# A top-k attention with two expert layers: the mask moves from VectorE to ScalarE and GpSimd, ahead of the exponential

## The chip, the cores and the metric

The kernel runs on one core of a Trainium2 chip. The core has TensorE (matrix products), VectorE, ScalarE and GpSimd (elementwise work), and SyncE, which issues the DMA transfers. Every engine works through its own instructions in the order in which they were written down; semaphores make it wait for others. The metric is device time in microseconds, of which less is better.

## The reference

Attention over q, k and v of shape (4, 8, 576, 64), in which each query keeps its 32 largest scores, then two expert layers on the 2304 tokens of 512 numbers:

```python
scores = scale * np.matmul(q, k.transpose(0, 1, 3, 2))
kth = np.partition(scores, -top_k, axis=-1)[..., -top_k:-top_k + 1]
scores = np.where(scores >= kth, scores, -1000000000.0)
scores = scores - np.max(scores, axis=-1, keepdims=True)
attn = np.exp(scores)
attn = attn / (np.sum(attn, axis=-1, keepdims=True) + 1e-09)
x = np.matmul(attn, v)                        # -> (2304, 512)
h = np.maximum(x @ w_in1, 0.0);  y = h * h @ w_out1
h = y @ w_in2;  out = (h * np.clip(h + 3.0, 0.0, 6.0) / 6.0) @ w_out2
```

The four weight matrices have 512 x 2048 or 2048 x 512 numbers and arrive as 64-bit words.

## The kernel before

**Numbers.** Every operand of a product is split into two f16 parts, a high and a low one, after a scaling by a power of two; each product is done as three (high-high, high-low, low-high). The scale of a matrix needs its largest column norm first: products of the matrix with itself (line 428), a reduction on VectorE (line 448), a transpose and a spread on TensorE (lines 471, 478). Then each slab of 128x512 is scaled and split, for the first, second and most of the third matrix by products with a diagonal on TensorE (lines 536, 542) and copies on ScalarE, for the rest by ScalarE and GpSimd (lines 518 to 524). The first and third matrix have four reductions, the second and fourth one. Before that VectorE turns 64-bit words into f32 (lines 362 to 365), and GpSimd adds the low bits (line 412). Slabs are loaded into space that later holds other matrices, so a load waits until the slab before it in its place is converted.

**Attention.** There are 4 x 5 blocks of (batch, up to 128 tokens): four full ones and a half one of 64 a batch. A full block has 8 tiles, one for each head, a half one has 4 with two heads each: 144 tiles of 128x576 scores. `attend` writes down a tile's steps: score products (line 764), the copy S to SBUF on ScalarE (770), seven steps on VectorE that find the 32 largest (maximum of eight, line 778 and 786; replacement of these in W, line 783), a bias on GpSimd (790), the exponential on ScalarE (795), the mask on VectorE, which multiplies the exponential by S >= the 32nd value and sums the row (801), the high part wc on ScalarE (806), the low part on GpSimd (810, 811), a DMA transpose of both to wT (815) and the value products (829). `x_operand` divides by the sums and transposes a block into the buffer hl, with which the first layer starts. `q_prep` and `kv_prep` load and scale q, k and v; the scale comes from `norm_tasks`: squares summed on ScalarE (line 595), a sum over the partitions by a product with ones on TensorE (599), and a scale on VectorE (261 to 263).

**Layers.** The two half blocks of neighbouring batches are joined, so there are 18 units of 128 tokens. `group` writes down a quarter of a layer of a unit: products into hb (line 1075), Relu and square, or Relu and gate (1082 to 1090), the high part on ScalarE (1097), the low part on GpSimd (1100), second products (1110 in the first layer, 1118 in the second). `x2_operand` turns the first layer's result into the second's operand, in the same buffer hl, which is free only after the second layer.

**Order.** None of this order is written out by hand. `task` notes each step with its engine, an estimated cost, a key, what it waits for, and the buffers that it takes; `free` says whose end gives a buffer back. `Plan.run` plays the steps through with these estimates: an engine that is free takes the ready step with the smallest key for which all buffers are there, and that is the order in which instructions are written. `lat` is what the planner counts between a step's end and the start of those that wait for it (2.0 us after a step of SyncE). The keys come from constants at the end of the file: `AKEY` for the tile's steps on ScalarE and GpSimd, `GKEY` for the groups, `WKEY` for weight loads, `CKEY` for conversions, `SKEY` and `SPL` for splits, `QKV` for the loads of q, k and v.

Of the kernel before, what the change touches and what calls it, by code (L numbers as in the profile page):

```python
# [9 lines left out]
F32 = mybir.dt.float32  # L10
F16 = mybir.dt.float16
# [8 lines left out]
P = 128  # L20
# [12 lines left out]
class Plan:  # L33
# [29 lines left out]
    def free(self, name, owner, *users):  # L63
        e = [len(users), name, owner]
        for u in users:
            u.rel.append(e)
# [66 lines left out]
def tile_topk_attention_moe_moe2(  # L133
# [55 lines left out]
    def pool(name, n, shape, dtype, where=None):  # L189

        plan.pool(**{name: n})
        size[name] = (shape, dtype, where or sb)
# [20 lines left out]
    acc_t = ps.tile([P, 2, 512], F32, name="acc")  # L213
    plan.pool(acc0=1, acc1=1)
    pool("S", SBUFS, [P, S], F32)
    pool("W", 2, [P, S], F32)
    pool("E", 2, [P, S], F32)
    pool("wc", 2, [P, 2 * S], F16)
    pool("wT", 2, [P, 2 * S // P, P], F16)
    pool("kn", 1, [P, 4 * NCH * D], F16)  # L220
    pool("qT", 2, [P, 8, P], F16)
    pool("kT", 4, [P, 2 * NCH, P], F16)
# [2 lines left out]
    pool("qf", 1, [P, 4, D], F32)  # L225
    pool("x", XBUFS, [P, H, D], F32)
    pool("f", FBUFS, [P, 512], F32)
    pool("hl", 2, [P, 2, KD, 2 * P], F16)
    pool("ghl", GBUFS, [P, 2, 512], F16)
    pool("m", 3, [P, TOPK], F32, st)  # L230
    pool("sums", 2, [P, H], F32, st)
    pool("rv", 2, [P, H], F32, st)
    pool("scl", 3, [P, 2], F32, st)
    for name, n in (("nb", 2), ("ss", 6), ("sck", 1), ("scv", 1), ("scq", 2), ("qinv", 2), ("xy", 2), ("scx", 6),
                    ("px", 6), ("sc2", 4), ("p2", 2), ("r", 6), ("pm", 2), ("sm", 2), ("ca", 2), ("oc", 2)):
        scalar(name, n)
    scalar("wmx", 4)
# [19 lines left out]
    def scale_pair(y_ap, inv, add, sc):  # L257

        e = scalars[:, size["e"] + nexp[0] % 4:size["e"] + nexp[0] % 4 + 1].bitcast(I32)
        nexp[0] += 1  # L260
        nc.vector.tensor_scalar(e, y_ap.bitcast(I32), EXPMASK, 1, op0=ALU.bitwise_and, op1=ALU.logical_shift_right)
        nc.vector.tensor_scalar(sc.bitcast(I32), e, -1.0, EXP_S, op0=ALU.mult, op1=ALU.add)
        nc.vector.tensor_scalar(inv.bitcast(I32), e, 1.0, add, op0=ALU.mult, op1=ALU.add)
# [320 lines left out]
    def when(kkey):  # L584
        return first[kkey[1]] + 2.0 * kkey[2] if kkey[0] == "q" else first[first_of(order, kkey[1])] + kkey[2]

    def norm_tasks(tag, src, junk, n, cost, deps, alloc, inv, kkey, reads=(), writes=()):

        box = {}

        def square():
            for a_ in alloc:
                T[a_, kkey] = take(a_)
            box["ss"] = take("ss")
            nc.scalar.activation(junk(), src(), AF.Square, accum_out=box["ss"][0:n])

        def total():
            box["pn"] = take("misc", "pn" + tag)
            nc.tensor.matmul(box["pn"][:, 0:1], ones32[0:n, :], box["ss"][0:n], start=True, stop=True)

        def scale():
            box["sc"] = take("sc" + tag)
            scale_pair(box["pn"][:, 0:1], inv(), EXP_I, box["sc"])

        t1 = task("ACT", cost, (PREP, when(kkey)), square, deps=deps, alloc=["ss", *alloc], reads=reads, writes=writes)
        t2 = task("PE", 0.2, (0, when(kkey)), total, deps=[t1], alloc=["misc"])
        t3 = task("DVE", 0.34, (0, when(kkey)), scale, deps=[t2],
                  alloc=["sc" + tag] + (["qinv"] if tag == "q" else []))
        free("ss", t1, t2)
        free("misc", t2, t3)  # L610
        return box, t1, t3

    def kv_prep(which, b, hp, deps):
# [73 lines left out]
    def q_prep(i, half):  # L687

        b, j = order[i]
        n = nof[i]  # L690
        box = {}
        own = (i, half) == (0, 1)
        rd = []
        if own:
            box["f"], rd = region(32768 - 16 * D, 16 * D, F32)
        kkey = ("q", i, half)

        def load():
# [12 lines left out]

        bx, t1, t3 = norm_tasks("q", lambda: box["f"][0:n].rearrange("p h d -> p (h d)"),
                                lambda: T["kn", kkey][0:n].bitcast(BF16)[:, 0:4 * D], n, 0.4, [l], ["kn", "qT"],
                                lambda: T.setdefault(("qinv", kkey), None) or T.__setitem__(("qinv", kkey), take("qinv"))
                                or T["qinv", kkey], kkey, reads=rd)

        def scales():
            T["scl", kkey] = take("scl")
            for c in range(2):
                hp = 2 * half + c  # L720
                nc.gpsimd.tensor_scalar(T["scl", kkey][:, c:c + 1], kvinv[:, 0, b % 2, hp:hp + 1],
                                        T["qinv", kkey][:, 0:1], 0.125, op0=ALU.mult, op1=ALU.mult)

        def flip():
            nc.sync.dma_start_transpose(out=T["qT", kkey][:, :, 0:n],
                                        in_=T["kn", kkey][0:n, 0:16 * D])

        lows = split(4 * D, lambda: box["f"][0:n], [lambda a=a: qn()[0:n, :, 0, a, :] for a in range(2)],
                     [lambda a=a: qn()[0:n, :, 1, a, :] for a in range(2)], lambda: bx["sc"][0:n], SQ if b else SQ0,
                     ((PREP, when(kkey)), (1, when(kkey))), [t3], rd)  # L730
        t5 = task("POOL", 0.5, (0, when(kkey)), scales, deps=[t3] + [kT_task[b, 2 * half + c][1] for c in range(2)],
                  alloc=["scl"])
        t6 = task("SP", 1.0, (0, when(kkey)), flip, deps=lows)
        free("scq", t3, *lows)
        free("qinv", t3, t5)
        free("kn", t1, t6)
        if not own:
            free("qf", l, *lows)
        qT_task[i, half], qT_use[i, half] = (t1, t6), []
        scl_use[i, half] = (t5, [])  # L740
# [10 lines left out]
    def attend(s):  # L751
# [38 lines left out]
            nc.gpsimd.tensor_scalar(T["nb", s], T["m", s][:, 0:1], T["scl", ("q", i, half)][:, hp % 2:hp % 2 + 1],  # L790
                                    -1.0, op0=ALU.mult, op1=ALU.mult)

        def expo():
            T["E", s] = take("E")
            nc.scalar.activation(T["E", s], T["S", s], AF.Exp, bias=T["nb", s],  # L795
                                 scale=T["scl", ("q", i, half)][:, hp % 2:hp % 2 + 1])

        def mask():
            if t == 0:
                T["sums", i] = take("sums")  # L800
            nc.vector.scalar_tensor_tensor(T["E", s], T["S", s], T["m", s][:, TOPK - 1:TOPK], T["E", s],  # L801
                                           op0=ALU.is_ge, op1=ALU.mult, accum_out=T["sums", i][:, t:t + 1])

        def high():
            T["wc", s] = take("wc")
# [33 lines left out]
        for r in range(7):  # L839
# [2 lines left out]
            ops.append(prev)  # L842
        free("W", ops[1], ops[6])
        tn = task("POOL", 0.25, (0, s), bias, deps=[ops[0], scl_use[i, half][0]], alloc=["nb"])
        te = task("ACT", 0.76, (AKEY[1], s), expo, deps=[tn, before[1]], alloc=["E"])
        free("nb", tn, te)
        scl_use[i, half][1].append(te)
        tm = task("DVE", 0.815, (2, s + 0.7), mask, port=True, deps=[ops[6], te, mask_task.get((i, 0))],
                  alloc=["sums"] if t == 0 else [])
        mask_task[i, t] = tm  # L850
        free("S", tb, tm)
        free("m", ops[0], tm)
        th = task("ACT", 0.57, (AKEY[2], s), high, deps=[tm, before[2]], alloc=["wc"])
        tl = task("POOL", 1.38, (AKEY[3], s), low, deps=[th, before[3]])
        free("E", te, tl)
        tw = task("SP", 1.25, (0, s), flip, deps=[tl, before[4]], alloc=["wT"])
        free("wc", th, tw)
        tv = task("PE", 0.44 if len(hs) == 1 else 0.9, (2, s), av, deps=[tw, vv_task[b, hp][1], before[5]],
                  alloc=["av"] if t == 0 else [])
        av_tasks[i, t] = tv  # L860
        tile_tasks.append((ta, te, th, tl, tw, tv))
        free("wT", tw, tv)
        vv_use[b, hp].append(tv)

# [398 lines left out]
SBUFS = 3  # L1263
FBUFS = 2
XBUFS = 1
GBUFS = 3
PREFILL = 1
SKV = 'd'
SQ = 'a'
SKV0 = 'a'  # L1270
SQ0 = 'a'
GKEY = (4, 1.5)
AKEY = (0.5, 1, 3, 3.5)
SX = 'a'
SX0 = 'a'
XKEY = 1.5
NPOOL = (4, 4, 4, 4)
QKV = 0
WKEY = ((45.68, 1), (153.74, 0.1), (14.48, 0.1), (62.46, 0.1))
SPE = ('eeee', 'eeee', 'eeea', 'aaaa')  # L1280
SPL = (3.5, 1.5, 0.5)
ADD = (0.5, 1)
PREP = 1.5
VKEY = 3

CKEY = ((-3.61, 0.14), (-69.99, 3.36), (-31.64, 0.91), (-0.36, 1.29))
SKEY = (0, 100, 200, 300)

_INS = ["q", "k", "v", "moe_w_in", "moe_w_out", "moe2_w_in", "moe2_w_out"]
_OUTS = [((2304, 512), "float32")]  # L1290
# [24 lines left out]
```

## Time and profile before

| | |
|---|---|
| median of 3 runs | 1236.63 us (1236.08 to 1240.48) |
| the profiled execution's own time | 1238.58 us |
| its span, first to last instruction | 1236.8 us |
| TensorE products, busy | 1074.3 us, 87% |
| VectorE busy | 1058.9 us, 86% |
| ScalarE busy | 825.4 us, 67% |
| GpSimd busy | 663.8 us, 54% |
| mean granted TensorE clock | 0.947 |

The profile is of one execution. "PE" is TensorE's products and "PEld" its weight loads, "DVE" VectorE, "ACT" ScalarE, "POOL" GpSimd. Busy is the time in which at least one instruction of the engine ran. A line such as L801 is a line of the kernel. In a wait the engine, the instruction and the line that waited stand left of the arrow, and right of it what came last of that for which it waited.

### The profile page before, as it was taken

Reading aid. Unit: us, or ns where it says so; the run is one execution under the profiler, and the core shown is the slowest. Engines: PE = TensorE matmul, PEld = TensorE weight load, DVE = VectorE, ACT = ScalarE, POOL = GpSimd, SP = SyncE. Lnnn points to the kernel's source line nnn. Section 1 sums busy time; section 2 is a strip of 40 time slices with the busy share of each in tenths; the row PEclk is TensorE's granted clock in tenths of the full one; section 3 lists DMA queues with packets and bytes.
Section 4 is the critical chain, followed back from the end, with each engine's and each line's share of the span. In section 5 each row is a group of like instructions: output and inputs, shape, how many; then the busy total and the mean of one; then the engine's idle time right before and its main releaser. Section 6 shows DMA issues by size and latency. Waiting matters only on the chain.

```text
span 1236.8 us, 36708 instructions
## 1 busy us (share of the span) xinstructions
PE 1074.3 (87%) x14856; PEld 879.4 (71%) x14856; DVE 1058.9 (86%) x2463; ACT 825.4 (67%) x1580; POOL 663.8 (54%) x969
## 2 busy tenths in 40 slices
PE   2484389878989999999899999999998999999998
PEld 2332147577679769877887888788767868978885
DVE  5999999999978999999999999999868989999011
ACT  7677588769767668666766757576866666755422
POOL 5857846458654556554545555655544555545312
PEclk9676599998999999999899999999998999999999
DMA  9989744333454233344574323435433233433100
GB/s 209 268 247 265 228 101 115 71 55 55 96 113 93 53 63 70 66 71 82 89 109 72 68 56 71 55 64 98 97 59 73 54 66 73 65 49 58 22 2 18
DMA packets 276762, 112.47 MB, mean 91 GB/s; under 512 B 257521, under 2 KB 265713, under 8 KB 276593
## 3 DMA queue, kind: packets, MB, share of 16 engines
q1 hardware_dynamic: 276592, 110.14, 43.3%
q8 instruction: 116, 1.90, 0.6%
q14 instruction: 54, 0.43, 0.1%
HBM read 48.23 MB, written 4.72 MB: 43 GB/s over the span
## 4 chain that ended last, share of the span: by engine, by line
PE 42%; DVE 15%; ACT 10%; DMA 10%; issue 5%; POOL 5%; SPq 1%; POOLq 0%; DVEq 0%; ACTq 0%
PE hb L1075 16%; PE acc L1118 9%; PE acc L1110 8%; DMA wT<-wc 8%; DVE W L783 4%; DVE m L786 4%; PE av L829 3%; PE sp L764 3%; DVE E L801 2%; DVE m L778 2%; POOL wc L810 1%; ACT E L795 1%; POOL ghl L1100 1%; ACT x L896 1%; ACT S L770 1%
## 5 line engine op out<-in xcount | busy, mean ns | idle before, releaser
L1075 PE MATMUL hb<-hl,w 128*128 128x128 f16 x6912 | 455.8, 220 | 3.7 <-ACT r L1082 2.2
L1075 PEld LDWEIGHTS <-w 128*128 128x128 f16 x6912 | 415.7, 99 | 42.8 <-issue 6.2
L786 DVE MAX8 m<-W 128x8 f32<-128x576 f32 x432 | 314.8, 747 | 0.2
L1100 POOL TENSOR_TENSOR ghl<-r,ghl 128x512 f16<-128x512 f32 x144 | 172.7, 1201 | 193.3 <-ACT ghl L1097 141.9
L1110 PE MATMUL acc<-ghl,w 128*128 128x128 f16 x3456 | 242.0, 221 | 9.9 <-POOL ghl L1100 4.2
L810 POOL TENSOR_TENSOR wc<-E,wc 128x512 f16<-128x512 f32 x144 | 167.8, 1165 | 145.2 <-ACT wc L806 117.8
L1118 PE MATMUL acc<-w,ghl 128*128 128x512 f16 x864 | 234.3, 382 | 2.8 <-POOL ghl L1100 1.5
L1110 PEld LDWEIGHTS <-w 128*128 128x128 f16 x3456 | 212.8, 99 | 29.8 <-issue 14.0
L783 DVE MATCH_REPLACE8 W<-m,W 128x576 f32<-128x576 f32 x288 | 213.3, 742 | 0.0
L795 ACT ACTIVATE E<-S,scalars,scl 128x576 f32<-128x576 f32 x144 | 124.8, 867 | 85.9 <-POOL scalars L790 65.3
L801 DVE SCALAR_TENSOR_TENSOR E<-S,m,E 128x576 f32<-128x576 f32 x144 | 137.2, 952 | 0.1
L770 ACT ACTIVATE S<-sp 128x576 f32<-128x576 f32 x144 | 92.9, 645 | 53.8 <-DVE E L801 40.9
L764 PE MATMUL sp<-kT,qT 128*128 128x288 f16 (+1 forms) x640 | 102.4, 303 | 25.0 <-ACT S L770 21.0
L829 PE MATMUL av<-vv,wT 128*128 128x64 f16 (+1 forms) x2240 | 92.7, 197 | 33.7 <-DMA wT<-wc 32.8
L829 PEld LDWEIGHTS <-wT 128*128 128x128 f16 (+1 forms) x2240 | 81.2, 103 | 56.5 <-DMA wT<-wc 46.9
L1097 ACT ACTIVATE ghl<-r 128x512 f16<-128x512 f32 x144 | 89.8, 626 | 40.9 <-PE acc L1110 21.2
L778 DVE MAX8 m<-S 128x8 f32<-128x576 f32 x144 | 107.3, 746 | 4.9 <-ACT S L770 4.9
L783 DVE MATCH_REPLACE8 W<-m,S 128x576 f32<-128x576 f32 x144 | 106.8, 741 | 0.0
L1118 PEld LDWEIGHTS <-ghl 128*128 128x128 f16 x864 | 73.8, 99 | 45.2 <-issue 3.3
L806 ACT ACTIVATE wc<-E 128x576 f16<-128x576 f32 x144 | 97.7, 679 | 4.6 <-DVE E L801 4.5
L412 POOL TENSOR_TENSOR w<-w,stg 128x512 int32<-128x512 int32 x57 | 73.0, 1294 | 35.4 <-DVE w L365 23.6
L1090 DVE SCALAR_TENSOR_TENSOR r<-r,hb 128x512 f32<-128x512 f32 x72 | 48.9, 680 | 49.6 <-ACT r L1084 49.4
(128 smaller groups left out, 1343.2 us busy)
## 6 DMA issues: line engine op xcount, KB each, us to landing
w<-in_moe_w_in_dram SPq DMA_DIRECT2D x32, 512.0 KB, 4.8
w<-in_moe_w_out_dram SPq DMA_DIRECT2D x29, 512.0 KB, 4.8
out_dram<-o SPq DMA_DIRECT2D x16, 256.0 KB, 2.4
qf<-in_q_dram SPq DMA_DIRECT2D x31, 128.0 KB, 3.1
stg<-in_k_dram SPq DMA_DIRECT2D x12, 256.0 KB, 3.2
stg<-in_v_dram SPq DMA_DIRECT2D x12, 256.0 KB, 3.1
wT<-wc SPq DMA_TRANSPOSE x144, 3.2
stg<-in_moe_w_out_dram SPq DMA_DIRECT2D x6, 256.0 KB, 3.9
```

Source lines behind the costliest of these rows:

```text
L764: nc.tensor.matmul(dst, qT[:, 2 * ((2 * hp + hh) % 4) + a, 0:M], kflat[:, hh * SPAD + c * HALF:hh * SPAD + (c + 1) * HALF], start=a == 0, ...
L778: nc.vector.max(m[:, 0:8], T["S", s])
L783: nc.vector.match_replace(out=T["W", s], in_to_replace=m[:, 8 * c - 8:8 * c], in_values=T["S", s] if c == 1 else T["W", s], imm_value=-3.0e38)
L786: nc.vector.max(m[:, 4 * r:4 * r + 8], T["W", s])
L795: nc.scalar.activation(T["E", s], T["S", s], AF.Exp, bias=T["nb", s], scale=T["scl", ("q", i, half)][:, hp % 2:hp % 2 + 1])
L801: nc.vector.scalar_tensor_tensor(T["E", s], T["S", s], T["m", s][:, TOPK - 1:TOPK], T["E", s], op0=ALU.is_ge, op1=ALU.mult, accum_out=T["s ...
L810: nc.gpsimd.tensor_tensor(wc[:, S + TAIL:], e[:, 0:S - TAIL], wc[:, 0:S - TAIL], op=ALU.subtract)
L829: nc.tensor.matmul(out_[cols, t * D:(t + 1) * D], wT[0:kr, a, cols], vv[0:kr, vb, hh, c, :], start=n_ == 0, stop=n_ == len(prods) - 1)
L1075: nc.tensor.matmul(box["h"][:, fi * n:(fi + 1) * n], wt[2 * m][:, kk * 4 + f // 4, a, f % 4 * P:(f % 4 + 1) * P], hl[:, c, kk, 0:n], start ...
L1100: nc.gpsimd.tensor_tensor(flat(box["g"][:, 1]), flat(box["r"]), flat(box["g"][:, 0]), op=ALU.subtract)
L1110: nc.tensor.matmul(flat_[:, c * w_:c * w_ + n], wt[1][:, f, a, c * P:(c + 1) * P], gl[d], start=(f, a, d) == (0, 0, 0) and c * w_ % 512 == ...
L1118: nc.tensor.matmul(o_, gl[d][:, ch * P:ch * P + rows], wt[3][:, f, a, :], start=f == 0 and (a, d) == (0, 0), stop=f == KF - 1 and (a, d) = ...
```

## The change

- The mask comes before the exponential. `lowest` on VectorE multiplies the 32nd value by 2^96 (128x1). `below` on ScalarE makes Relu(2^96 x (32nd value - S)), which is 0 for a score that stays and huge for one that doesn't. `mask` on GpSimd subtracts that from S. The exponential works on the result in place and sums the row itself. S is freed by the subtraction, E is taken by the Relu. The scale of q is kept above 2^-56.
- W has one buffer instead of two, wT three instead of two, m four instead of three, nb three instead of two.
- hl has four buffers of 128 tokens instead of two of 256.
- For a full block of q the scale is taken for each token from its own sum of squares, and the sum over the partitions on TensorE falls away. The factor of 1/8 moves into the scale's exponent.
- The planner counts 4.5 us after a transpose of wT instead of 2.0.
- The constants of the keys are others; among them weight loads of the second matrix (83.47 and up) now come before those of the third (106.39 and up) where both can be issued; before it was 153.74 and 14.48.

```diff
-    pool("W", 2, [P, S], F32)
+    pool("W", 1, [P, S], F32)
-    pool("wT", 2, [P, 2 * S // P, P], F16)
+    pool("wT", WTB, [P, 2 * S // P, P], F16)
-    pool("hl", 2, [P, 2, KD, 2 * P], F16)
+    pool("hl", HBUFS, [P, 2, KD, P], F16)
-    pool("m", 3, [P, TOPK], F32, st)
+    pool("m", 4, [P, TOPK], F32, st)
...
-            scale_pair(box["pn"][:, 0:1], inv(), EXP_I, box["sc"])
+            scale_pair(box["ss"] if rows else box["pn"][:, 0:1], inv(), EXP_I - (3 << 23) * (tag == "q"), box["sc"])
...
-        t2 = task("PE", 0.2, (0, when(kkey)), total, deps=[t1], alloc=["misc"])
+        rows = tag == "q" and n == P
+        t2 = t1 if rows else task("PE", 0.2, (0, when(kkey)), total, deps=[t1], alloc=["misc"])
...
-                                        T["qinv", kkey][:, 0:1], 0.125, op0=ALU.mult, op1=ALU.mult)
+                                        T["qinv", kkey][:, 0:1], SCLMIN, op0=ALU.mult, op1=ALU.max)
...
+        def lowest():
+            T["kb", s] = take("kb")
+            nc.vector.tensor_scalar(T["kb", s], T["m", s][:, TOPK - 1:TOPK], FAR, None, op0=ALU.mult)
+        def below():
+            T["E", s] = take("E")
+            nc.scalar.activation(T["E", s], T["S", s], AF.Relu, bias=T["kb", s], scale=-FAR)
+        def mask():
+            nc.gpsimd.tensor_tensor(T["E", s], T["S", s], T["E", s], op=ALU.subtract)
         def expo():
-            T["E", s] = take("E")
-            nc.scalar.activation(T["E", s], T["S", s], AF.Exp, bias=T["nb", s],
-                                 scale=T["scl", ("q", i, half)][:, hp % 2:hp % 2 + 1])
-        def mask():
             if t == 0:
                 T["sums", i] = take("sums")
-            nc.vector.scalar_tensor_tensor(T["E", s], T["S", s], T["m", s][:, TOPK - 1:TOPK], T["E", s],
-                                           op0=ALU.is_ge, op1=ALU.mult, accum_out=T["sums", i][:, t:t + 1])
+            nc.scalar.activation(T["E", s], T["E", s], AF.Exp, bias=T["nb", s],
+                                 scale=T["scl", ("q", i, half)][:, hp % 2:hp % 2 + 1],
+                                 accum_out=T["sums", i][:, t:t + 1])
...
-        te = task("ACT", 0.76, (AKEY[1], s), expo, deps=[tn, before[1]], alloc=["E"])
+        tk = task("DVE", 0.07, (2, s + 0.7), lowest, deps=[ops[6]], alloc=["kb"])
+        tr = task("ACT", 0.68, (AKEY[1], s), below, deps=[tk, before[1]], alloc=["E"])
+        tm = task("POOL", 1.24, (MKEY, s), mask, deps=[tr])
+        free("S", tb, tm)
+        te = task("ACT", 0.96, (AKEY[1], s), expo, deps=[tn, tm, mask_task.get((i, 0))],
+                  alloc=["sums"] if t == 0 else [])
-        tm = task("DVE", 0.815, (2, s + 0.7), mask, port=True, deps=[ops[6], te, mask_task.get((i, 0))],
-                  alloc=["sums"] if t == 0 else [])
-        th = task("ACT", 0.57, (AKEY[2], s), high, deps=[tm, before[2]], alloc=["wc"])
+        th = task("ACT", 0.57, (AKEY[2], s), high, deps=[te, before[2]], alloc=["wc"])
-        tw = task("SP", 1.25, (0, s), flip, deps=[tl, before[4]], alloc=["wT"])
+        tw = task("SP", 1.25, (0, s), flip, deps=[tl, before[4]], alloc=["wT"], lat=WLAT)
...
-GKEY = (4, 1.5)
-AKEY = (0.5, 1, 3, 3.5)
+HBUFS = 4
+GKEY = (29.26, 13.13)
+AKEY = (0.09, 0.66, 4.41, 4.29)
-XKEY = 1.5
+XKEY = 0.69
-QKV = 0
-WKEY = ((45.68, 1), (153.74, 0.1), (14.48, 0.1), (62.46, 0.1))
+QKV = 4.45
+WKEY = ((36.97, 0.08), (83.47, 0.18), (106.39, 0.2), (97.4, 0.05))
-SPL = (3.5, 1.5, 0.5)
-ADD = (0.5, 1)
-PREP = 1.5
-VKEY = 3
-CKEY = ((-3.61, 0.14), (-69.99, 3.36), (-31.64, 0.91), (-0.36, 1.29))
-SKEY = (0, 100, 200, 300)
+SPL = (3.28, 0.06, 0.06)
+ADD = (-4.32, 0.86)
+PREP = 1.7
+VKEY = 1.86
+MKEY = -1.12
+WLAT = 4.5
+WTB = 3
+NBUFS = 3
+FAR = 2.0 ** 96
+SCLMIN = 2.0 ** -56
+CKEY = ((-6.41, 0.38), (-66.39, 4.6), (-35.42, 1.18), (-0.72, 1.02))
+SKEY = (1.34, 112.21, 208.36, 272.85)
```

## Rows read from the trace of the kernel before

**Rows 1.** Busy time by stretch (us from the start): engines, granted clock, DMA share, GB/s.

```profile
0.00:155.00 155.00, 71.28 (x414) 41.99 (x415) 134.50 (x292) 102.45 (x190) 108.56 (x133) 0.71 0.88 243
155.00:1145.00 990.00, 917.93 (x13281) 767.66 (x13279) 913.60 (x2146) 690.20 (x1333) 533.48 (x816) 0.98 0.41 74
1145.00:1237.00 92.00, 85.12 (x1169) 69.73 (x1165) 10.76 (x26) 32.70 (x58) 21.73 (x22) 0.99 0.07 13
sum 1237.00, PE 1074.33 PEld 879.38 DVE 1058.86 ACT 825.35 POOL 663.77; mean PE 358.11 PEld 293.13 DVE 352.95 ACT 275.12 POOL 221.26
```

**Rows 2.** Waits, whole span: us in total, times, the longest in us.

```profile
ACT E L795 <- POOL scalars L790: 65.3, 44, 3.4
...
PE acc L428 <- POOL w L412: 44.2, 14, 13.0
...
ACT S L770 <- DVE E L801: 40.9, 31, 3.7
...
PE av L829 <- DMA wT<-wc: 32.8, 32, 2.3
...
PE sp L764 <- ACT S L770: 21.0, 12, 4.1
```

**Rows 3.** Groups by line and shape: count, busy us, mean ns, idle before.

```profile
L810 POOL TENSOR_TENSOR wc<-E,wc 128x512 f16<-128x512 f32 x144 | 167.8, 1165 | 145.2 <-ACT wc L806 117.8 <-DVE m L778 15.3 <-issue 5.6
L801 DVE SCALAR_TENSOR_TENSOR E<-S,m,E 128x576 f32<-128x576 f32 x144 | 137.2, 952 | 0.1
L795 ACT ACTIVATE E<-S,scalars,scl 128x576 f32<-128x576 f32 x144 | 124.8, 867 | 85.9 <-POOL scalars L790 65.3 <-POOL wc L811 20.3
...
L806 ACT ACTIVATE wc<-E 128x576 f16<-128x576 f32 x144 | 97.7, 679 | 4.6 <-DVE E L801 4.5
...
L412 POOL TENSOR_TENSOR w<-w,stg 128x512 int32<-128x512 int32 x57 | 73.0, 1294 | 35.4 <-DVE w L365 23.6 <-ACT stg L408 6.1 <-DVE scalars L466 2.3
...
L811 POOL TENSOR_TENSOR wc<-E,wc 128x64 f16<-128x64 f32 x144 | 50.2, 349 | 0.0
...
L262 DVE TENSOR_SCALAR scalars<-scalars 128x1 int32<-128x1 int32 x114 | 17.5, 153 | 4.2
...
L801 DVE DVE_READ_ACCUMULATOR E<-S,m,E 128x1 f32 x144 | 11.6, 80 | 0.0
...
L595 ACT ACTIVATION_READ_ACCUMULATOR kn<-qf 128x1 f32 x31 | 6.0, 194 | 0.0
```

**Rows 4.** VectorE in order of time: start us, us, instruction, near 607 and 1141.

```profile
607.60 0.74 DVE L783 MATCH_REPLACE8 W<-m,W 128x576 f32<-128x576 f32 x1
608.26 0.08 DVE L783 MATCH_VALUE_LOAD W<-m,W 128x8 f32 x1
...
1141.13 0.74 DVE L783 MATCH_REPLACE8 W<-m,W 128x576 f32<-128x576 f32 x1
1141.91 0.76 DVE L786 MAX8 m<-W 128x8 f32<-128x576 f32 x1
```

**Rows 5.** Groups by line and shape: q's sum over the partitions on TensorE.

```profile
L599 PE MATMUL pnq<-scalars,ones 128*128 128x1 f32 x64 | 11.7, 252 | 7.9 <-ACT kn L595 7.9
...
L599 PEld LDWEIGHTS pnq<-scalars,ones 128*128 128x128 f32 x64 | 11.3, 215 | 10.0 <-ACT kn L595 5.2 <-issue 4.2
```

**Rows 6.** DMA issues by line: count, median us from issue to landing.

```profile
wT<-wc SPq DMA_TRANSPOSE x144, 3.2
```

**Rows 7.** Busy time in one stretch, columns as in the first group.

```profile
100.00:155.00 55.00, 17.79 (x119) 11.24 (x119) 53.36 (x105) 31.02 (x58) 45.66 (x48) 0.53 0.82 246
```

**Rows 8.** Single instructions: reductions of line 448 (min/median/max ns, first and last), then by time.

```profile
L448 DVE TENSOR_REDUCE scalars<-acc x10: 672/684/692, 32.0 to 260.8; 128x1 f32<-128x512 f32 x10
...
146.58 0.68 DVE L448 TENSOR_REDUCE scalars<-acc 128x1 f32<-128x512 f32 x1
...
271.89 1.75 ACT L896 ACTIVATE x<-av,rv 128x64 f32<-128x64 f32 x8
...
316.36 0.66 PE L905 MATMUL pt<-ident,x 128*128 128x128 f32 x4
```

More of the change, by code (lines that the diff above doesn't have):

```diff
@@ L233, in tile_topk_attention_moe_moe2 @@
     pool("scl", 3, [P, 2], F32, st)
-    for name, n in (("nb", 2), ("ss", 6), ("sck", 1), ("scv", 1), ("scq", 2), ("qinv", 2), ("xy", 2), ("scx", 6),
+    for name, n in (("nb", NBUFS), ("kb", 2), ("ss", 6), ("sck", 1), ("scv", 1), ("scq", 2), ("qinv", 2), ("xy", 2), ("scx", 6),
                     ("px", 6), ("sc2", 4), ("p2", 2), ("r", 6), ("pm", 2), ("sm", 2), ("ca", 2), ("oc", 2)):
@@ L602, in scale @@
             box["sc"] = take("sc" + tag)
-            scale_pair(box["pn"][:, 0:1], inv(), EXP_I, box["sc"])
+            scale_pair(box["ss"] if rows else box["pn"][:, 0:1], inv(), EXP_I - (3 << 23) * (tag == "q"), box["sc"])
         t1 = task("ACT", cost, (PREP, when(kkey)), square, deps=deps, alloc=["ss", *alloc], reads=reads, writes=writes)
-        t2 = task("PE", 0.2, (0, when(kkey)), total, deps=[t1], alloc=["misc"])
+        rows = tag == "q" and n == P
+        t2 = t1 if rows else task("PE", 0.2, (0, when(kkey)), total, deps=[t1], alloc=["misc"])
         t3 = task("DVE", 0.34, (0, when(kkey)), scale, deps=[t2],
                   alloc=["sc" + tag] + (["qinv"] if tag == "q" else []))
-        free("ss", t1, t2)
-        free("misc", t2, t3)
+        free("ss", t1, t3 if rows else t2)
+        if not rows:
+            free("misc", t2, t3)
         return box, t1, t3
@@ L844, in attend @@
         tn = task("POOL", 0.25, (0, s), bias, deps=[ops[0], scl_use[i, half][0]], alloc=["nb"])
-        te = task("ACT", 0.76, (AKEY[1], s), expo, deps=[tn, before[1]], alloc=["E"])
+        tk = task("DVE", 0.07, (2, s + 0.7), lowest, deps=[ops[6]], alloc=["kb"])
+        free("m", ops[0], tk, tn)
+        tr = task("ACT", 0.68, (AKEY[1], s), below, deps=[tk, before[1]], alloc=["E"])
+        free("kb", tk, tr)
+        tm = task("POOL", 1.24, (MKEY, s), mask, deps=[tr])
+        free("S", tb, tm)
+        te = task("ACT", 0.96, (AKEY[1], s), expo, deps=[tn, tm, mask_task.get((i, 0))],
+                  alloc=["sums"] if t == 0 else [])
         free("nb", tn, te)
         scl_use[i, half][1].append(te)
-        tm = task("DVE", 0.815, (2, s + 0.7), mask, port=True, deps=[ops[6], te, mask_task.get((i, 0))],
-                  alloc=["sums"] if t == 0 else [])
-        mask_task[i, t] = tm
-        free("S", tb, tm)
-        free("m", ops[0], tm)
-        th = task("ACT", 0.57, (AKEY[2], s), high, deps=[tm, before[2]], alloc=["wc"])
+        mask_task[i, t] = te
+        th = task("ACT", 0.57, (AKEY[2], s), high, deps=[te, before[2]], alloc=["wc"])
         tl = task("POOL", 1.38, (AKEY[3], s), low, deps=[th, before[3]])
-        free("E", te, tl)
-        tw = task("SP", 1.25, (0, s), flip, deps=[tl, before[4]], alloc=["wT"])
+        free("E", tr, tl)
+        tw = task("SP", 1.25, (0, s), flip, deps=[tl, before[4]], alloc=["wT"], lat=WLAT)
         free("wc", th, tw)
@@ L860, in attend @@
         av_tasks[i, t] = tv
-        tile_tasks.append((ta, te, th, tl, tw, tv))
+        tile_tasks.append((ta, tr, th, tl, tw, tv))
         free("wT", tw, tv)
```

## The prediction

> **What bounds the kernel now.** I read the stretches first (which engine is busy when), then what ends TensorE's idle time, then single groups of instructions.
>
> Over the span TensorE works 1074 us and VectorE 1059, ScalarE 825, GpSimd 664. In 0 to 155 us TensorE works 71 us and idles 84, while VectorE is busy 134 of 155: weights are being converted and TensorE has little to do. From 155 to 1145 TensorE works 918 of 990 us (idle 72) and VectorE 914. In the last 92 us only products of the two layers are left: TensorE 85 us, VectorE 11 [rows 1]. So the time is TensorE's 1074 us of work, plus 162.5 us of idle time, plus 1.8 us around the span: 1238.6, the profiled execution's own time, 1.9 above the median of 1236.6. An edit matters only where it takes work from TensorE or fills its idle time; a faster VectorE does so only where TensorE waits behind it.
>
> What ends the idle time [rows 2]: 44 us (14 waits) before the products that measure the weights, for GpSimd's integer add; 33 us (32 waits of at most 2.3) before the value product, for the transposed weights wT; 21 us before the score product, for the copy S. The last has a further cause: ScalarE's copy S waits 41 us for VectorE's mask, which holds the S buffer.
>
> **The change part by part.**
>
> *Mask off VectorE.* Out go 144 masks of 0.952 us and their accumulator reads of 0.080, 137 + 12 = 149 us. In come 144 products of 128x1 at about 0.15, the price of the 128x1 step on line 262: 22 us [rows 3]. Net -127 us.
>
> *One W buffer instead of two* gives part of it back. Now two tiles alternate on VectorE: after the replacement at 607.60 the next instruction, another tile's, starts at 608.26, 0.66 us later. Where one tile ran alone, the replacement at 1141.13 is followed by its own maximum at 1141.91, 0.78 later [rows 4]. A dependent step costs 0.12 us more. A tile has six such steps; with one W only the next tile's first maximum, a gate, a scale or a conversion can come between. Bounds: 0, and 6 x 0.12 x 144 = 104 us. I take half the gaps filled, 52 us, so VectorE's net relief is 75 us (23 to 127). It is busy 1048 us up to 1145, 91.5%; 973 us at that share is 1063, less than TensorE needs below. VectorE then no longer sets the pace, though not by much.
>
> *ScalarE* gets a Relu with one pointer operand over 128x576. The pass without a pointer (line 806) takes 0.679, with two (line 795) 0.867; between them 0.77, 111 us. The exponential now writes an accumulator, whose read takes 0.194: 28 us [rows 3]. 825 + 139 = 964 us, 82% of the forecast.
>
> *GpSimd* gets a subtraction of 128x576. 512 columns take 1.165 and 64 take 0.349, so 1.8 ns a column and 1.28 for 576; from the add that writes 32-bit words (1.294 for 512) 1.41 [rows 3]. 184 to 203 us; I take 184, the row that is also a subtraction of f32 tiles. 664 + 184 = 848 us, 72%.
>
> Neither engine is over, so in the sum both cost nothing: idle time of the two between tiles hides them. If that cover goes, TensorE waits for the groups behind them (a rival below).
>
> *The waits that this adds.* The Relu waits for VectorE's 128x1 product, GpSimd's subtraction for the Relu, ScalarE's exponential for the subtraction. Behind the exponential on ScalarE stand the Relu, square and copy of the layers' groups and the copy S; behind the subtraction on GpSimd the groups' low parts. TensorE's second products wait for these. One wait goes: the copy to wc now follows ScalarE's own exponential, not VectorE.
>
> The Trainium skill speaks against this move: its page "GPSIMD Engine Reference", section 4.1 Engine selection, sends elementwise work on a tile to VectorE and puts GpSimd at about half its speed with two inputs. The rows agree on the price (1.28 + 0.77 + 0.19 us in place of VectorE's 1.03), and by that rule the change should lose; the time for that is the ScalarE rival's below, about 1249.
>
> *q scaled per token.* 64 products of 128x1 leave TensorE with their 64 weight loads (the 16 of half tiles stay): 11.7 us of products, 11.3 of loads [rows 5]. Bounds 0 (all in idle time) and -23; a quarter lies in the early idle time and loads overlap other products: **-10**.
>
> *Third wT buffer, and the planner counts 4.5 us after a transpose instead of 2.0.* The transpose lands a median 3.2 us after its issue [rows 6], later than the plan thought, and so TensorE stands before the value product for 33 us. With the longer figure the written order puts products of the layers there, and with a third buffer a late value product doesn't hold the next transpose. Bounds 0 and -33; two thirds, as some waits come where the layers have nothing ready: **-22**.
>
> *Order of the weights.* Between 100 and 155 us TensorE works 18 of 55 us at a granted clock of 0.53 (between its two levels), VectorE 53, and the DMA engines are 82% busy [rows 7]. The second matrix's one reduction, which ends its measuring, runs at 146.58 [rows 8]; only then can its split (34 products) and the first unit's first layer start. Slabs of the third are loaded and converted in the meantime. With the second ahead, its split and a first layer move into that idle time. What each moved load brings along is one DMA on SP's queue and VectorE's conversion; the q, k and v loads are later in key by 4.45, so weights pass some of them. Bounds 0 (what is left waits for the fourth matrix, whose reduction at 260.8 gates the second layer) and -37 (all idle time of 100 to 155). No row tells how much of that idle time the order alone fills, and VectorE, busy there nearly throughout, must first find the time; its masks of these tiles go too. I take half the bound: **-18**.
>
> *Four operand buffers.* The third block is copied out at 271.89, but transposed on TensorE only at 316.36 [rows 8]: both buffers are taken until the first unit's second layer has run. Four buffers let the third unit's first layer start some 40 us sooner. TensorE has other work at that place (it idles 72 us in all of 155 to 1145), so this is a part of the -18 and not a term; the bytes are the same.
>
> *S is held to the subtraction instead of the mask.* 21 us of TensorE's waits hang on the copy S. Bounds -21 and +21: VectorE is late less often, but the new holder comes two handovers later in the tile. **-5**, as three S buffers stay.
>
> The scalars' extra buffers, the fourth m and the lower limit of the scale cost nothing: they add no instruction.
>
> The sum: 1238.6 - 10 - 22 - 18 - 5 = 1183.6, less 1.9 to the median: **1182 us**. TensorE's idle time would be some 118 us instead of 162.
>
> **The rivals.**
>
> *VectorE stays the pace* (one W, no gap filled). Relief 23 us: 1025 at 91.5% is 1120 instead of 1145, so -25 with all other gains drowned in it: 1238.6 - 25 - 1.9 = 1212. If the six waits also push the Relu back, up to 1230. For it: two tiles alternate in most of the trace. Against: gates, scales and conversions come between.
>
> *Slower: ScalarE held up by the subtraction.* ScalarE works 690 us in 155 to 1145 [rows 1]; 134 tiles add 134 x 0.96 = 129, so 819. Each exponential stands in order until GpSimd is done. Today's exponential waited 65.3 us in 44 cases for a GpSimd scalar, 1.5 each [rows 2]. If every tile's did so: 819 + 201 = 1020 us, 30 more than the 990 of now: 1238.6 - 18 + 30 - 1.9 = 1249. It decides from (990 - 819) / 134 = 1.28 us of wait a tile. Against it: the written order can put other work between, and only 44 of 144 waited.
>
> *The order of loads does nothing*, because loads wait for staging space and VectorE's order still favours the third matrix: 1182 + 18 = 1200, inside the forecast's range.
>
> *All idle time goes that can*: -37, -33, -21 and the -10: 1238.6 - 101 - 1.9 = 1136.
>
> **How the numbers follow.** The forecast's case, 1165 to 1212: 0.55. Best case, under 1165: 0.13. VectorE still the pace, 1212 to 1230: 0.14. Nearly nothing left of it, 1230 to 1243: 0.06. Slower by ScalarE, over 1243: 0.12. About 0.5%, 6 us, is what can be told from no change. Faster 0.55 + 0.13 + 0.14 = 0.82, same 0.06, slower 0.12. The range 1145 to 1234 leaves out the slow case and the far end of the best.
>
> **What would show it.** Right: line 801's mask gone and VectorE's busy time near 932; a Relu near 0.77, a subtraction near 1.28; ScalarE near 964, GpSimd near 848, TensorE near 1063; the value product's waits for wT near 11 us; the second matrix's reduction well before 147. Wrong: exponentials that wait over 1.28 us a tile for the subtraction (slower rival); dependent steps 0.78 apart nearly everywhere, and VectorE idle for nothing else (W); 44 us of waits on GpSimd's add still there (order of loads). The forecast fails most easily if TensorE's idle time after 155 us changes its cause but not its sum.

## The result: 1189 us, 4% faster, and the profile after

The changed kernel takes 1188.97 us (median, 1186.38 to 1190.16) against 1238.56 for the kernel before, measured beside it: a ratio of 0.960, 95% interval 0.957 to 0.963. The forecast was 1182 us in a range of 1145 to 1234. The profiled execution took 1190.16 us with a span of 1188.4.

The busy shares of the changed kernel, from its page:

```profile
PE 1059.1 (89%) x14792; PEld 865.8 (73%) x14792; DVE 986.4 (83%) x2319; ACT 926.0 (78%) x1868; POOL 834.5 (70%) x1113
```

The span is 48.4 us shorter: TensorE's busy time is 15.2 us less (1074.3 to 1059.1) and its idle time 33.2 us less (162.5 to 129.3). Where the idle time went is seen by stretch, columns as in [rows 1]; the last row again begins 92 us before the end:

```profile
0.00:155.00 155.00, 85.18 (x487) 48.27 (x488) 128.84 (x288) 117.12 (x227) 116.60 (x140) 0.85 0.79 230
155.00:1097.00 942.00, 890.09 (x13119) 746.66 (x13118) 848.31 (x2009) 779.15 (x1594) 698.20 (x956) 0.99 0.44 81
1097.00:1189.00 92.00, 83.81 (x1191) 70.84 (x1189) 9.29 (x24) 29.72 (x49) 19.74 (x19) 0.99 0.03 10
```

TensorE idles 70 us in the first 155 (84 before), 52 in the middle (72 before) and 8 in the last 92 (7 before). VectorE is still busy 90% of the middle (848 of 942; before 914 of 990, 92%): relieved, but no more than that.

The waits of the changed kernel that answer to [rows 2]; there is no row any more for the value product and wT:

```profile
ACT S L773 <- POOL E L806: 51.0, 51, 2.9
...
PE acc L428 <- POOL w L412: 30.2, 16, 5.1
PE sp L767 <- ACT S L773: 28.7, 28, 6.0
...
ACT E L811 <- POOL E L806: 1.8, 3, 0.9
```

So 33 us of waits for wT went, 14 of 44 before the products that measure the weights, and the score product waits 8 us longer than before for the copy S, which now waits for GpSimd's subtraction instead of VectorE's mask. The exponential, in which the slower rival would have shown, waits 1.8 us for the subtraction in all.

The groups that answer to [rows 3]:

```profile
L806 POOL TENSOR_TENSOR E<-S,E 128x576 f32<-128x576 f32 x144 | 203.1, 1411 | 49.0 <-ACT E L803 45.7 <-PE acc L1132 1.7 <-PE pnk L599 0.6
L811 ACT ACTIVATE E<-E,scalars,scl 128x576 f32<-128x576 f32 x144 | 124.4, 864 | 2.0 <-POOL E L806 1.8
L803 ACT ACTIVATE E<-S,scalars 128x576 f32<-128x576 f32 x144 | 111.4, 774 | 23.4 <-DVE scalars L798 20.1 <-POOL wc L822 2.6
...
L811 ACT ACTIVATION_READ_ACCUMULATOR E<-E,scalars,scl 128x1 f32 x144 | 28.3, 197 | 0.0
...
L798 DVE TENSOR_SCALAR scalars<-m 128x1 f32<-128x1 f32 x144 | 21.4, 148 | 2.8
```

The Relu took 0.774 us (forecast 0.77), the read of the sums 0.197 (0.194), VectorE's product 0.148 (0.15). The subtraction took 1.411: the upper bound that was named, not the 1.28 that was taken.

And single instructions of the changed kernel that answer to [rows 8]: the second matrix's reduction, the first products of the first unit, the third block's transpose:

```profile
123.78 0.68 DVE L448 TENSOR_REDUCE scalars<-acc 128x1 f32<-128x512 f32 x1
...
197.93 1.28 PE L1089 MATMUL hb<-hl,w 128*128 128x128 f16 x20 [0.68 <-DVE w L365]
...
278.31 1.56 PE L919 MATMUL pt<-ident,x 128*128 128x128 f32 x4
```

The reduction comes 23 us sooner, the third block's transpose 38 us sooner. But the first unit starts later (in the kernel before its first product ran at 179.4 us). By 325 us, where each kernel is about to store its first unit, TensorE has idled 107 us before and 101 after, and has done about the same number of products (2231 and 2244): the early stretch gave only 6 us of idle time. The rest came after it.

### The profile page after: what moved, and what is told of

Same layout as the page of the kernel before. It is cut to its first block, busy times and chain, and to the rows that moved or that the text cites. A ratio compares the mean times of both kernels' runs of the same rounds, so it can differ in the third digit from the quotient of the medians.

```text
span 1188.4 us, 36913 instructions
## 1 busy us (share of the span) xinstructions
PE 1059.1 (89%) x14792; PEld 865.8 (73%) x14792; DVE 986.4 (83%) x2319; ACT 926.0 (78%) x1868; POOL 834.5 (70%) x1113
## 4 chain that ended last, share of the span: by engine, by line
PE 43%; DVE 17%; ACT 16%; POOL 13%; issue 6%; DMA 3%; SPq 1%; POOLq 0%; ACTq 0%; DVEq 0%
PE hb L1089 16%; PE acc L1132 12%; PE acc L1124 6%; DVE W L786 5%; DVE m L789 5%; POOL E L806 4%; PE sp L767 3%; POOL wc L821 3%; PE av L840 2%; ACT E L811 2%; DVE m L781 2%; POOL ghl L1114 2%; ACT S L773 2%; ACT E L803 2%; DVE cv L362 2%
## 5 line engine op out<-in xcount | busy, mean ns | idle before, releaser
L1089 PEld LDWEIGHTS <-w 128*128 128x128 f16 x6912 | 415.1, 98 | 51.0 <-issue 7.4
L789 DVE MAX8 m<-W 128x8 f32<-128x576 f32 x432 | 326.1, 755 | 8.1
L1114 POOL TENSOR_TENSOR ghl<-r,ghl 128x512 f16<-128x512 f32 x144 | 169.3, 1178 | 104.9 <-ACT ghl L1111 92.2
L1124 PE MATMUL acc<-ghl,w 128*128 128x128 f16 x3456 | 238.7, 219 | 2.8 <-POOL ghl L1114 1.1
L806 POOL TENSOR_TENSOR E<-S,E 128x576 f32<-128x576 f32 x144 | 203.1, 1411 | 49.0 <-ACT E L803 45.7
L1124 PEld LDWEIGHTS <-w 128*128 128x128 f16 x3456 | 206.7, 98 | 16.2 <-issue 5.3
L803 ACT ACTIVATE E<-S,scalars 128x576 f32<-128x576 f32 x144 | 111.4, 774 | 23.4 <-DVE scalars L798 20.1
L767 PE MATMUL sp<-kT,qT 128*128 128x288 f16 (+1 forms) x640 | 100.1, 299 | 32.1 <-ACT S L773 28.7
L811 ACT ACTIVATE E<-E,scalars,scl 128x576 f32<-128x576 f32 x144 | 124.4, 864 | 2.0 <-POOL E L806 1.8
L767 PEld LDWEIGHTS <-qT 128*128 128x128 f16 (+1 forms) x640 | 55.5, 103 | 62.7 <-issue 44.8
L1098 ACT ACTIVATE r<-hb,bias,scalars 128x512 f32<-128x512 f32 x72 | 55.8, 775 | 54.4 <-PE hb L1089 53.3
```

The costliest lines, as they stand in the source:

```text
L767: nc.tensor.matmul(dst, qT[:, 2 * ((2 * hp + hh) % 4) + a, 0:M], kflat[:, hh * SPAD + c * HALF:hh * SPAD + (c + 1) * HALF], start=a == 0, ...
L789: nc.vector.max(m[:, 4 * r:4 * r + 8], T["W", s])
L803: nc.scalar.activation(T["E", s], T["S", s], AF.Relu, bias=T["kb", s], scale=-FAR)
L806: nc.gpsimd.tensor_tensor(T["E", s], T["S", s], T["E", s], op=ALU.subtract)
L811: nc.scalar.activation(T["E", s], T["E", s], AF.Exp, bias=T["nb", s], scale=T["scl", ("q", i, half)][:, hp % 2:hp % 2 + 1], accum_out=T["s ...
L1089: nc.tensor.matmul(box["h"][:, fi * n:(fi + 1) * n], wt[2 * m][:, kk * 4 + f // 4, a, f % 4 * P:(f % 4 + 1) * P], hl[:, c, kk, 0:n], start ...
```

## The experiments

Theory T says that TensorE's wait for the transposes was the limit, rival V that VectorE's full time was; theory B, formed on the first four runs, that both were, side by side. All were run beside the kernel before, whose medians were 1236.0 to 1237.4. For each I give the time, TensorE's idle time up to 325 us (where weights are prepared), and from 325 to 1000 us (the steady stretch, 675 us less its busy time).

| kernel | us | ratio to before, interval | idle to 325 | idle 325 to 1000 |
|---|---|---|---|---|
| before | 1237 | | 107 | 43 |
| e1 before, 4.5 us after a transpose | 1215.0 | 0.981 (0.976 to 0.986) | 100 | 34 |
| e2 before, mask moved | 1262.3 | 1.019 (1.014 to 1.025) | 119 | 38 |
| e5 before, both | 1222.3 | 0.988 (0.986 to 0.991) | 114 | 26 |
| e11 before, another order | 1228.9 | 0.994 (0.993 to 0.996) | 96 | 39 |
| changed kernel | 1189.0 | 0.960 (0.957 to 0.963) | 101 | 18 |
| e3 changed, 2.0 us after a transpose | 1230.6 | 0.994 (0.991 to 0.997) | 108 | 38 |
| e4 changed, mask on VectorE | 1234.5 | 0.997 (0.995 to 1.000) | 101 | 46 |
| e6 changed, old keys | 1238.5 | 1.001 (0.998 to 1.004) | 128 | 32 |
| e7 changed, two W and two wT | 1212.7 | 0.980 (0.978 to 0.983) | 106 | 30 |
| e8 changed, q's sum on TensorE | 1210.9 | 0.980 (0.977 to 0.982) | 112 | 16 |
| e9 changed, another order | 1215.6 | 0.984 (0.982 to 0.987) | 112 | 26 |
| e10 changed, another order | 1202.5 | 0.974 (0.972 to 0.976) | 103 | 27 |
| e12 changed, two operand buffers | 1208.8 | 0.979 (0.977 to 0.980) | 104 | 29 |

The idle times are those of the one profiled execution, whose own time lies up to 6.5 us off the median (e3 and e6). The rows behind them, columns as in [rows 1], first of the kernel before, then of the changed one:

```profile
0.00:325.00 325.00, 218.04 (x2231) 153.67 (x2232) 297.48 (x663) 239.09 (x449) 206.78 (x271) 0.84 0.62 158
325.00:1000.00 675.00, 631.96 (x9432) 539.80 (x9433) 612.42 (x1463) 462.88 (x911) 358.81 (x562) 0.98 0.42 76
```

```profile
0.00:325.00 325.00, 224.12 (x2244) 153.38 (x2245) 288.56 (x660) 265.60 (x522) 251.89 (x316) 0.89 0.61 160
325.00:1000.00 675.00, 657.42 (x9918) 560.65 (x9916) 610.33 (x1458) 557.41 (x1152) 495.86 (x693) 1.00 0.45 80
```

**e1, the planner's figure for a transpose alone.**

```diff
-        tw = task("SP", 1.25, (0, s), flip, deps=[tl, before[4]], alloc=["wT"])
+        tw = task("SP", 1.25, (0, s), flip, deps=[tl, before[4]], alloc=["wT"], lat=4.5)
```

> The kernel before with one edit: the planner counts 4.5 us after a transpose of wT instead of 2.0; every instruction is the same, only their order differs. Theory T (the time went because TensorE no longer stands before the value product): the 33 us of waits for wT go, and the time falls by 20 to 33 us, to about 1210. Rival V (the time went because VectorE was relieved of the mask): VectorE does what it did, so 1232 to 1240.

1215.0, 22 us less, as theory T had it: the order that follows from one figure in the planner, with no other instruction, is worth that. (e11 below, another order of the same instructions without that figure, is worth 8.) The waits for wT fall from 32.8 to 2.5 us (e1's waits):

```profile
PE av L829 <- DMA wT<-wc: 2.5, 2, 2.2
```

But the steady stretch has only 9 us less idle time, and there VectorE is now busy 638 of 675 us, 95%:

```profile
325.00:1000.00 675.00, 640.54 (x9684) 551.67 (x9681) 638.30 (x1526) 476.57 (x936) 366.98 (x582) 0.99 0.43 77
```

**e2, the mask alone**, with two W buffers, old keys and the old figure (steps as in the diff of the change, key 0 for the subtraction, three buffers for the bias and four for the maxima).

```diff
...
+        tr = task("ACT", 0.68, (AKEY[1], s), below, deps=[tk, before[1]], alloc=["E"])
...
+        tm = task("POOL", 1.24, (MKEY, s), mask, deps=[tr])
...
-        tm = task("DVE", 0.815, (2, s + 0.7), mask, port=True, deps=[ops[6], te, mask_task.get((i, 0))],
...
```

> The kernel before with the mask moved alone: the 128x1 product, Relu on ScalarE, subtraction on GpSimd, exponential with its own row sum; two W buffers as before, so that two tiles can alternate on VectorE, two wT buffers, the old keys and the old 2.0 us after a transpose (one more buffer for the bias, the maxima; key 0 for the subtraction). Theory T: TensorE still waits for wT (about 33 us), VectorE's 127 us of relief are off the path: within 10 us of the kernel before. Rival V: 1195 to 1215.

1262.3, 25 us more, worse than either theory said. Its rows say where. VectorE is relieved (568 of 675 us in the steady stretch), and the waits for wT are nearly as they were (28.6 us). The steady stretch of e2, and its wait:

```profile
325.00:1000.00 675.00, 637.02 (x9501) 541.72 (x9499) 568.25 (x1429) 540.86 (x1116) 478.93 (x675) 0.99 0.43 78
```

```profile
PE av L837 <- DMA wT<-wc: 28.6, 25, 3.6
```

The loss lies before 325 us, where TensorE has done 1919 products instead of 2231; from there on e2 does its other 12937 in 932.9 us and the kernel before its 12625 in 911.8, 0.072 us each in both. Before 325 us GpSimd is busy 248 us instead of 207, ScalarE 260 instead of 239, and the first unit starts only here (e2 in order of time):

```profile
231.82 1.50 PE L1086 MATMUL hb<-hl,w 128*128 128x128 f16 x24 [0.77 <-ACT w L545]
```

What released it is ScalarE's copy of a split weight (line 545). So the tile's new steps, which these two engines do in their order, seem to come at the cost of the preparation of the weights; that is read from the busy times, and no run shifts these steps alone.

**e3 and e4, one part undone in the changed kernel.** In e4 the mask's steps are those of the kernel before, with two W and two wT buffers.

```diff
-        tw = task("SP", 1.25, (0, s), flip, deps=[tl, before[4]], alloc=["wT"], lat=WLAT)
+        tw = task("SP", 1.25, (0, s), flip, deps=[tl, before[4]], alloc=["wT"])
```

> The changed kernel with one edit: the planner counts 2.0 us after a transpose of wT again. Theory T: waits for wT come back, 20 to 30 us of them, and the time rises to 1209 to 1219 (less if the third wT buffer hides part). Rival V: 1186 to 1194.

> The changed kernel with the mask back on VectorE behind the exponential, and W and wT with two buffers each as before; all else (keys, four operand buffers, q scaled per token, 4.5 us after a transpose) as in the changed kernel. Theory T: few of the 48 us come back, 1189 to 1200. Rival V: VectorE is again busy over 91% of the time up to the last tile, 1215 to 1235.

1230.6 and 1234.5: each alone takes back nearly all of the 48 us. Neither T nor V can say so. In e3 the waits for wT are back (the third wT buffer hides nothing of them). In e4 VectorE is busy 619 of 675 us; that is little more than the 610 of the changed kernel, so the busy share by itself doesn't show that VectorE held TensorE back. First e3's wait and steady stretch, then e4's steady stretch:

```profile
PE av L840 <- DMA wT<-wc: 38.3, 33, 7.1
...
325.00:1000.00 675.00, 636.64 (x9347) 532.45 (x9348) 584.48 (x1387) 536.26 (x1100) 476.96 (x662) 0.99 0.43 78
```

```profile
325.00:1000.00 675.00, 628.51 (x9303) 536.29 (x9301) 618.80 (x1483) 461.71 (x909) 358.98 (x564) 0.97 0.42 77
```

e4 undoes two buffer counts (W and wT) together with the mask. e7 below undoes these counts alone (1212.7), so that the mask's steps by themselves are the 22 us from e7 to e4, and TensorE's steady idle time goes from 30 to 46 us between the two.

**e5, both edits on the kernel before** (the diffs of e1 and e2 together).

> The kernel before with the mask moved (as in e2) and 4.5 us counted after a transpose (as in e1), all keys old. Theory B (two limits side by side: TensorE's wait for wT and VectorE's full time each hold the steady stretch, so that either edit alone gives little there and both together much): TensorE's idle time from 325 to 1000 us falls from 34 (e1) and 38 (e2) to 25 or less, and the time to 1215 to 1235, though the late start of e2 stays. Additive rival: e2's 1262 less the 22 of e1, 1236 to 1248.

1222.3, and TensorE's idle time in the steady stretch is 26 us (43 before, 34 and 38 with one edit), where theory B wanted 25 or less:

```profile
325.00:1000.00 675.00, 649.06 (x9767) 554.19 (x9766) 587.35 (x1456) 549.91 (x1139) 491.40 (x685) 1.00 0.43 80
```

By these four runs alone B isn't shown: the two single effects, added, would leave 29 us, and another order of the same steps moves this idle time by 4 us (e11) or 9 (e10). The fourteen kernels together bear it out: 39 and 43 us with neither part, 34 to 46 in the four with one of them (e1 to e4), 16 to 32 in the eight with both. What B says of the reason, that VectorE's full time is the second limit, stays argued. e4's trace shows part of the way from the mask on VectorE to TensorE. TensorE waits there for GpSimd's low parts of the groups (e4's wait, whole span):

```profile
PE acc L1113 <- POOL ghl L1103: 14.7, 8, 2.7
```

In e7 that is 3.4 us, in the changed kernel 1.1, and in e4 GpSimd's low parts in turn wait 10.4 us for VectorE's mask. But in the kernel before, with its mask on VectorE too, it is 4.2 only, and the 10.4 fit VectorE's full time as well as single late masks, a rival that no run separates from it.

The late start of e2 is still there (114 us idle by 325), so the whole is worse than e1 alone.

**e6, the old keys in the changed kernel.**

```diff
-WKEY = ((36.97, 0.08), (83.47, 0.18), (106.39, 0.2), (97.4, 0.05))
+WKEY = ((45.68, 1), (153.74, 0.1), (14.48, 0.1), (62.46, 0.1))
...
```

(and GKEY, AKEY, XKEY, QKV, SPL, ADD, PREP, VKEY, CKEY, SKEY in the same way.)

> The changed kernel with all keys of before (the order constants of ScalarE's, GpSimd's and TensorE's steps, of loads, conversions and splits), its buffers, steps and 4.5 us kept. Theory K (the keys repair the early stretch, where the moved mask delays the weights on GpSimd and ScalarE): by 325 us the layers are as late as in e2, 15 to 25 us behind, and the time is 1205 to 1225. Rival (the keys are a detail): 1183 to 1195.

1238.5, no faster than the kernel before. By 325 us TensorE has idled 128 us (e6's early stretch):

```profile
0.00:325.00 325.00, 196.91 (x1801) 132.61 (x1802) 288.22 (x648) 256.94 (x508) 246.38 (x311) 0.83 0.61 159
```

1801 products instead of the changed kernel's 2244. The layers don't start late here, as they do in e2 and e5 (232 and 228 us): a first quarter runs at 187 us, sooner than in the changed kernel (198). But it stands alone, and the first unit is stored only at 355 us instead of 325. The time lies outside both cases: the keys do more than expected.

**e7 and e8, two more parts undone.**

```diff
-    pool("W", 1, [P, S], F32)
+    pool("W", 2, [P, S], F32)
...
-WTB = 3
+WTB = 2
```

> The changed kernel with two W buffers and two wT buffers, as before. If one W costs what VectorE's rows say (some 54 us of busy time by steps that follow their own tile's) and VectorE is still near the pace: VectorE busy near 932 instead of 986 and the time 1170 to 1184. If VectorE is off the path, or the third wT buffer is worth as much: 1184 to 1196. If the third wT buffer is what frees TensorE: over 1200, with the waits for wT back.

```diff
-        rows = tag == "q" and n == P
+        rows = False
```

> The changed kernel with the sum over the partitions for q back on TensorE (64 products of 128x1 and their 64 weight loads). The prediction's term: 10 us more, 1195 to 1203, TensorE busy near 1071. If the products lie in idle time: 1184 to 1192.

1212.7 and 1210.9, 24 and 22 us slower than the changed kernel, e8 above both of its cases. In e7 the waits for wT are not back (0.7 us), and VectorE's busy time is 946.9 instead of 986.4, so one W does cost VectorE 40 us. Less work on VectorE and a slower kernel: that fits none of the three cases. It raised the question what a new order alone is worth.

**e9, e10 and e11, another order of the same steps.** One estimate of the planner is moved by 5 or 10 ns; no step, buffer or key differs.

```diff
-        prev = task("DVE", 0.73 if r % 2 else 0.667, (2, s + 0.1 * r), lambda r=r: topk(r), deps=[prev],
+        prev = task("DVE", 0.73 if r % 2 else 0.672, (2, s + 0.1 * r), lambda r=r: topk(r), deps=[prev],
...
```

(e9 on the changed kernel, e11 on the kernel before; in e10 the bias counts 0.26 instead of 0.25.)

> The changed kernel with the planner's estimate of a maximum at 0.672 us instead of 0.667; no step, buffer or key differs, only the written order. If single undone parts cost what they cost because of the part (theory P): 1183 to 1195. If any new order of the same steps loses the same 20 us (theory O: the keys fit this one order): 1203 to 1220.

> The changed kernel with the planner's estimate of the bias at 0.26 us instead of 0.25, again nothing but another order. Theory P: 1183 to 1195. Theory O: 1203 to 1220.

> The kernel before with the planner's estimate of a maximum at 0.672 us instead of 0.667. Theory P: 1231 to 1243. Theory O, if the old keys had been fitted to one order too: 1245 to 1260; if they had not, either way by up to 20 us.

1215.6 and 1202.5: the changed kernel loses 27 and 13 us by a new order of the same steps. The kernel before gains 8 (1228.9). So its own order was not the best one, while the changed kernel's is the fastest of the three orders run of it. By these two nudges, few as they are, what an edit costs in the changed kernel can be told from a new order only above some 27 us. By that measure e3 (42 us), e4 (46, mask and buffers together) and e6 (50) stand; e7, e8, e12 and the 22 us from e7 to e4 don't. e3 and e6 are themselves nothing but other orders of the changed kernel's steps; what sets e3 apart is that its loss shows as waits for wT.

**e12, two operand buffers.**

```diff
-HBUFS = 4
+HBUFS = 2
```

> The changed kernel with two operand buffers of 128 tokens instead of four. Theory P with the prediction's reading (the third unit's first layer can start some 40 us sooner, worth little): the third block's transpose on TensorE comes only after the first unit's second layer (about 320 us instead of 279), 1189 to 1200. Theory O: 1203 to 1220, with the same third transpose.

1208.8, within what a new order does. The third block's transpose comes at 305 us instead of 278 (e12 in order of time):

```profile
305.02 0.60 PE L919 MATMUL pt<-ident,x 128*128 128x128 f32 x4
```

So the two more buffers do let the third unit begin sooner; what that is worth stays open. Not tried: a mask on ScalarE and GpSimd that gives way to the weights until they are ready.

## Why the prediction was right, step by step

The time was 7 us above the forecast, and its case was the right one. TensorE's idle time is 129 us instead of 118, its busy time 1059 instead of 1063. The sum behind it was right in the mechanism of one term, the waits for wT, and owes the rest to errors that cancelled. That it came so near is in part luck: two other orders of the same steps (e9, e10) lie 34 and 20 us above the forecast.

*Waits for wT, -22.* Right in mechanism: the planner counted too little after a transpose. Alone the edit gave 22 us and took 30 of the 33 us of waits (e1); in the changed kernel all went, and without the figure they are back (e3). Another order alone took 11 of them (21.8 left in e11). What the prediction lacked is that this term depends on the mask's: in the steady stretch the kernels with one of the two parts idle 34 to 46 us, hardly less than those with neither (39 and 43), and those with both 16 to 32. The terms of two such parts can't be added.

*VectorE's relief, no term.* The forecast put no time on it, since TensorE was the bound. That was the step that failed: with the mask on VectorE again and the buffer counts of before the kernel takes 1234.5 (e4), 46 us more, beyond what the nudges did; 24 us of these come with the buffer counts alone (e7). The prediction saw VectorE busy 914 of 990 us, took TensorE for the bound and gave VectorE's relief no time. But of TensorE's steady idle time 43 us stood in that kernel and 34 in e1, where VectorE filled 95%; only with the mask gone as well did it fall to 26 (e5). Why the mask's place counts, by VectorE's full time or by single late masks, stays open.

*One W.* Taken at 52 us of VectorE's time, it cost 40 (986.4 in the changed kernel against 946.9 in e7). It shows as busy time, not as gaps, which is most of why the 932 us that were forecast didn't come: instructions of two tiles overlap at their ends, those of one tile don't. (With two W in e7 it is still 946.9; these 15 us were not followed.) The row of the changed kernel that answers to [rows 4] has the next instruction 0.77 us after the replacement's start:

```profile
618.51 0.74 DVE L786 MATCH_REPLACE8 W<-m,W 128x576 f32<-128x576 f32 x1
619.28 0.76 DVE L789 MAX8 m<-W 128x8 f32<-128x576 f32 x1
```

*ScalarE and GpSimd at no cost.* Wrong in the early stretch. Their busy times came near the forecast (926 for 964, as neighbouring ScalarE instructions overlap by 0.1 us; 834.5 for 848, though the subtraction was dearer), and after 325 us there was room. Before it there seems to have been none: the mask alone made the kernel 25 us slower (e2). That is not the mechanism of the slower rival, for the exponential waits for the subtraction 1.0 us in all in e2 and 1.8 in the changed kernel. The Trainium skill ("GPSIMD Engine Reference", section 4.1 Engine selection) sends elementwise work to VectorE and puts GpSimd at about twice VectorE's time with two inputs. e2 went the way of that rule; the changed kernel, with the same steps on GpSimd, didn't (1189 us against 1237), and of single instructions GpSimd's subtraction takes 1.411 us where VectorE's mask took 0.952, 1.5 times.

*Order of the weights, -18.* The size failed. The reduction came 23 us sooner and TensorE worked 36 instead of 18 us between 100 and 155; the idle time of 0 to 155 fell by 14 us. The split (48 products, not 34) moved there, but the first unit's first layer did not: it began at 198 us instead of 179, and by 325 us only 6 us were left. The other runs say what the keys do there: with the mask on VectorE TensorE idles 96 to 107 us by 325 (before, e1, e4, e11), with the mask moved and the old keys 114 to 128 (e2, e5, e6), with the mask moved and the new keys 101 to 112 (seven kernels). So the keys about pay for the mask; the prediction counted them as a gain.

*q, -10.* The products that left TensorE had taken 11.7 us. Its busy time fell by 15.2, but it is 1059.1, 1070.5 and 1060.5 us in three orders of the same products (the changed kernel, e9, e10), so that the two can't be set against each other. In time e8 can't be told from a new order, so the term is open.

*S, -5.* It went the other way, 21.0 to 28.7 us of waits, within its bounds.

*The order itself.* No term at all, and none of the rivals: 13 to 27 us of the 48 are gone when the same steps are written in another order. The two orders of the kernel before lie at 1237 and 1229, those of the changed one at 1189, 1203 and 1216. The whole change is worth some 13 to 48 us by these five. Against e1 (1215.0), which has of the change only the planner's figure, all the rest of it (mask, buffers, keys, q) is worth 26, 13 and -1 us in the three orders. How much of the order was found with the keys and how much was chance can't be told from so few.

## What to carry to other kernels

Where two engines are each over 90% busy, as TensorE and VectorE were here from 155 to 1145 us, an edit that helps one may show little, or a loss, until the other is helped too: test the edits alone and together before adding their gains. If a planner writes the order, compare its figures with the trace (2.0 us counted, 3.2 landed) before moving work, since correcting a figure is free, and the order that came of it was 22 us faster here. And nudge some of its estimates by a few per cent first: the spread of those runs, up to 27 us in two nudges here, is the least that a single undone part must cost before it says anything.

## What the runs showed that was not expected

A subtraction of f32 tiles into f32 took GpSimd 1.411 us for 576 columns in every case, 2.45 ns a column, while one into f16 took 1.171 for 512, 2.29 a column; by the two f16 rows' slope 1.28 had been expected. ScalarE paid less than the instructions' own durations: each begins 0.1 us before the one ahead of it ends, so adding 140 us of instructions (111.4 and 28.3) raised its busy time by 101 (825.4 to 926.0). Three of them in order of time:

```profile
700.63 0.87 ACT L811 ACTIVATE E<-E,scalars,scl 128x576 f32<-128x576 f32 x1
701.39 0.20 ACT L811 ACTIVATION_READ_ACCUMULATOR E<-E,scalars,scl 128x1 f32 x1
701.48 0.69 ACT L273 ACTIVATE hl<-acc,scalars 128x512 f16<-128x512 f32 x1
```

The mask of the kernel before has 0.952 us for its mean but 0.81 for its median (min, median and max in ns, then the first and last start):

```profile
L801 DVE SCALAR_TENSOR_TENSOR E<-S,m,E x144: 793/810/2440, 36.5 to 1142.8; 128x576 f32<-128x576 f32 x144
```

In that trace the mask is long where it meets GpSimd. Where one of GpSimd's two-input tensor instructions had over 0.5 us left as the mask began, 29 of 30 masks took over 0.9 us (mean 1.45); where none was running, none of 94 did (mean 0.81). One mask starts at 736.71 us and takes 1.72, beside a group's low part that GpSimd runs from 736.66 to 737.82. In all 35 masks take over 0.9 us, 20.5 us together above the median. So part of what the mask cost VectorE came with GpSimd's work; no run tests it.
